# Attention in float32 by head pairs on halves of TensorE's rows and columns, with a float32 first input product in batch 0

## The chip, the cores and the metric

The kernel runs on one core of one Trainium2 chip. The metric is the time of one execution on the device, in microseconds. The time of before is 1350.27 us, the median of three runs (1349.99 to 1351.18).

## The reference

There are 4 batches, 12 heads, a sequence of 448 and a head size of 64. For each head:

```python
scores = scale * np.matmul(q, k.transpose(0, 1, 3, 2))
scores = cap * np.tanh(scores / cap)
scores = scores - np.max(scores, axis=-1, keepdims=True)
attn = np.exp(scores)
attn = attn / (np.sum(attn, axis=-1, keepdims=True) + 1e-09)
out = np.matmul(attn, v)
```

The heads' outputs side by side are a matrix x of 1792 rows and 768 columns. Two layers follow, each with an input product (768 to 2048), a pointwise function and an output product (2048 to 768): `h - tanh(h)` in the first, `h * sigmoid(1.702 h)` in the second. Activations come as float32, the weights as float64. The result is float32.

## The kernel before, in words

Everything is kept transposed: features on the 128 partitions, the 448 positions of a batch along the free dimension. The kernel works batch by batch. `attention()` (L491) is a generator over all 48 heads that stops at each batch's end; the loop at L723 goes through the products of one batch (`moe`, L680: input and output product of layer one, then of layer two) and after each matrix product counts up `owed` by the rates of L32, and takes a step of the attention of the next batch whenever a full step is owed (L730 to L734). In the first quarter of batch 0's products the rate is 0. Batch 0's own attention runs alone before it (L709). The program is then put in order per engine by a scheduler, which keeps this priority but lets work go ahead that is ready, such as weight conversions during batch 0's attention.

**Precision.** TensorE multiplies either float32 or a rounded form of it that takes fewer passes. The kernel mostly uses the rounded form three times: a number is split into a high part (`hi_act`, `hi_dve`, L93 to L97) and the rest (`lo_dve`, `lo_pool`, L99 to L103), and high by high, high by low and low by high are added up. So `gemm_in` (L619) makes 18 products of 128 x 128 by 128 x 448 for each of its 16 blocks f, and `gemm_out` (L640) 48 for each of its 6 blocks e. A block of `gemm_in` takes its PSUM bank from the pool `ps_m` (two banks), in later batches every fourth from `ps_s` (L622).

**Weights.** In batch 0 each of 68 chunks of weights comes as float64 (`dbl_dma`, L159, three buffers `wd`), is made float32 by two steps of ScalarE and two of VectorE (`w_convert`, L189, three buffers `wr`), is written back to HBM for later batches (`kept`, L203), and is split into `wh` and `wl` (`w_split`, L206, three buffers each): the high part on VectorE or ScalarE, the low part on GpSimd in batch 0 and on VectorE later. `ahead` (L573) asks for the chunk that is needed two blocks later.

**Attention before.** A pair g is two heads. `load_qk` (L238) and `load_v` (L250) load it. For pairs 0 and 1 `pt_head` (L263) transposes q and k of each head to 64 rows of float32, and `qk` (L323) makes the scores in float32. For all other pairs q and k are transposed, split into high and low (`th`, `tl`, L289 and L290), and put on top of each other by 12 transfers (`pt_stack`, L292: `qs`, `kh`, `kl`), so that two products over 128 rows give the scores of one chunk of 112 queries. `tanh_max` (L345) takes the tanh and the row maximum of two chunks; `exps` (L362) makes the exponentials, with row sums from the same instruction; `norm` (L372) divides, on VectorE and GpSimd, except in batch 0, where the division is left for the output. `p_trans` (L394) transposes the probabilities and copies them (`pf`) in batch 0 or splits them (`ph`, `pl`) later. `pv` (L422) multiplies by v: in batch 0 in float32, both heads on halves of TensorE's columns; later by eight products per head, with v split by `v_split` (L312). `pv_out` (L447) writes x, in batch 0 with its split (`xh`, `xl`, L463 and L464). PSUM tiles of attention come from `ps_b` (two tiles of two banks, and a third from `ps_f` in batch 0, L130) and from `ps_s` (two banks).

## Time and profile before

| | |
|---|---|
| median of three runs | 1350.27 us |
| the profiled execution | 1349.97 us |
| its span (first to last instruction) | 1348.2 us |
| TensorE busy in the span | 1265.4 us, 94% |
| VectorE / ScalarE / GpSimd busy | 950.5 / 911.1 / 383.9 us |
| mean granted TensorE clock | 0.976 of 2.4 GHz |
| moved by DMA | 235 MB, 174 GB/s |

The span is what the profile sees of the execution. An engine's busy share is a mean over stages that differ much. Matrix products overlap, and their ends are modelled, so that the mean duration of one (370 ns for 448 columns) is longer than the distance to the next.

### The profile page before, as it was taken

To read this page: it belongs to the slowest core of one execution; us is meant where nothing else is said; L and a number is where in the kernel's file an instruction comes from. 1 tells how busy PE (TensorE), PEld (TensorE's weight loads), DVE (VectorE), ACT (ScalarE), POOL (GpSimd) and SP (SyncE) were. 2 spreads that over 40 slices of the span, in tenths; PEclk is the share of its full clock that TensorE was granted. 3 is DMA by queue.
4 is the path that set the end of the run, shared out by engine and by line. 5 is a ranking of instruction groups with operands and counts; after the bars stand their busy time and mean duration, and the time that the engine had idled before them with its cause. 6 is when DMAs were issued, how large, how long until landed. Compare 5 with 4: busy or idle time off the path is not lost.

```text
span 1348.2 us, 19078 instructions
## 1 busy us (share of the span) xinstructions
PE 1265.4 (94%) x6484; PEld 1109.9 (82%) x6484; DVE 950.5 (70%) x1338; ACT 911.1 (68%) x1466; POOL 383.9 (28%) x298
## 2 busy tenths in 40 slices
PE   8988778889888899999999999999999999999998
PEld 4556666778777788799999999999999999999997
DVE  5787999877888869976677727976767528834432
ACT  6986788888889869766777627866666527633421
POOL 1103556445674333310133102310132003201300
PEclk7999899899999899999999999999999999999999
DMA  7675556887778778665555566555543367433342
GB/s 202 169 180 149 174 168 212 240 269 238 205 251 244 216 229 300 250 184 152 142 150 140 158 186 204 149 149 143 151 133 109 96 181 215 130 116 112 105 118 59
DMA packets 170225, 235.23 MB, mean 174 GB/s; under 512 B 14224, under 2 KB 127120, under 8 KB 170128
## 3 DMA queue, kind: packets, MB, share of 16 engines
q1 hardware_dynamic: 170128, 234.02, 58.4%
q8 instruction: 51, 0.84, 0.3%
q14 instruction: 46, 0.38, 0.1%
HBM read 157.68 MB, written 46.01 MB: 151 GB/s over the span
## 4 chain that ended last, share of the span: by engine, by line
PE 61%; ACT 3%; DVE 3%; DMA 2%; issue 1%; SPq 1%; DVEq 0%; ACTq 0%
PE ps_y L648 27%; PE ps_h L628 23%; PE ps_pv L441 3%; PE ps_sc L339 3%; PE ps_pt L408 3%; DMA kept<-wr 1%; PE ps_o L671 1%; ACT wd L197 1%; PE ps_qk L279 1%; ACT t L367 0%; DMA wd<-in_moe_w_out_dram 0%; ACT wh L94 0%; DVE wl L100 0%; DMA wr<-kept 0%; DVE wr L199 0%
## 5 line engine op out<-in xcount | busy, mean ns | idle before, releaser
L628 PE MATMUL ps_h<-xh,wh 128*128 128x448 f32 x768 | 287.4, 374 | 37.3 <-DVE g_far L585 20.7
L648 PE MATMUL ps_y<-gh,wh 128*128 128x448 f32 x768 | 284.2, 370 | 7.3 <-DVE gh L97 2.4
L628 PE MATMUL ps_h<-xl,wh 128*128 128x448 f32 x768 | 285.7, 372 | 2.3 <-DVE xl L100 2.3
L648 PE MATMUL ps_y<-gl,wh 128*128 128x448 f32 x768 | 286.3, 373 | 0.2 <-POOL gl L103 0.2
L100 DVE TENSOR_TENSOR wl<-wr,wh 128x768 fp32r<-128x768 f32 (+1 forms) x172 | 157.8, 920 | 156.2 <-PE ps_y L648 84.5
L94 ACT CAST wh<-wr 128x768 fp32r<-128x768 f32 (+1 forms) x195 | 153.1, 787 | 158.6 <-PE ps_y L648 111.7
L628 PEld LDWEIGHTS ps_h<-xh,wh 128*128 128x128 f32 x768 | 146.4, 191 | 58.5 <-DVE g_far L585 24.4
L648 PE MATMUL ps_y<-gh,wl 128*128 128x448 f32 x768 | 188.6, 372 | 0.0
L628 PE MATMUL ps_h<-xh,wl 128*128 128x448 f32 x768 | 185.2, 371 | 0.0
L103 POOL TENSOR_TENSOR wl<-wr,wh 128x768 fp32r<-128x768 f32 (+1 forms) x68 | 130.4, 1918 | 136.1 <-DVE wh L97 82.0
L367 ACT ACTIVATE t<-t,tm,cpos 112x448 f32<-112x448 f32 x192 | 144.5, 756 | 34.5 <-DVE tm L358 34.3
L103 POOL TENSOR_TENSOR gl<-g_q,gh 128x448 fp32r<-128x448 f32 x64 | 90.4, 1413 | 262.0 <-ACT gh L94 166.8
L648 PEld LDWEIGHTS ps_y<-gh,wh 128*128 128x128 f32 x768 | 145.1, 189 | 20.5 <-DVE gh L97 2.7
L628 PEld LDWEIGHTS ps_h<-xl,wh 128*128 128x128 f32 x768 | 146.5, 191 | 15.4 <-DVE xl L100 2.8
L628 PEld LDWEIGHTS ps_h<-xh,wl 128*128 128x128 f32 x768 | 145.4, 191 | 12.7 <-DVE wl L100 0.4
L648 PEld LDWEIGHTS ps_y<-gh,wl 128*128 128x128 f32 x768 | 145.3, 191 | 12.1
L648 PEld LDWEIGHTS ps_y<-gl,wh 128*128 128x128 f32 x768 | 145.3, 189 | 12.0 <-POOL gl L103 0.7
L103 POOL TENSOR_TENSOR gl<-g_g,gh 128x448 fp32r<-128x448 f32 x64 | 79.6, 1244 | 199.5 <-DVE gh L97 66.1
L354 DVE TENSOR_REDUCE tm<-t 112x2 f32<-112x896 f32 x96 | 102.9, 1080 | 42.6 <-ACT t L350 42.3
L390 POOL TENSOR_SCALAR t<-t,rr 112x448 f32<-112x448 f32 x72 | 68.2, 957 | 215.2 <-DVE rr L377 162.6
L350 ACT ACTIVATE t<-ps_sc,tsc 112x896 f32<-112x896 f32 x96 | 95.8, 1010 | 48.0 <-PE ps_sc L339 43.7
L197 ACT ACTIVATE wd<-wd 128x768 uint16<-128x768 uint16 (+1 forms) x68 | 125.6, 1851 | 0.5
(84 smaller groups left out, 1909.5 us busy)
## 6 DMA issues: line engine op xcount, KB each, us to landing
wr<-kept SPq DMA_DIRECT2D x100, 384.0 KB, 3.2
wd<-in_moe_w_in_dram SPq DMA_DIRECT2D x64, 384.0 KB, 4.4
wr<-kept SPq DMA_DIRECT2D x72, 320.0 KB, 2.9
wd<-in_moe_w_out_dram SPq DMA_DIRECT2D x48, 384.0 KB, 4.5
kept<-wr SPq DMA_DIRECT2D x44, 384.0 KB, 5.0
wh<-kept_hl SPq DMA_DIRECT2D x32, 384.0 KB, 3.3
wl<-kept_hl SPq DMA_DIRECT2D x32, 384.0 KB, 3.7
kh<-th SPq DMA_DIRECT2D x88, 112.0 KB, 2.3
```

Of the source, the lines that this page charges most:

```text
L94: nc.scalar.copy(out=dst, in_=src)
L100: nc.vector.tensor_tensor(out=dst, in0=src, in1=hi.bitcast(F32), op=ALU.subtract)
L103: nc.gpsimd.tensor_tensor(out=dst, in0=src, in1=hi.bitcast(F32), op=ALU.subtract)
L197: nc.scalar.mul(out=half[:, :, :, 2], in_=half[:, :, :, 1], mul=F64_LOW)
L339: nc.tensor.matmul(ps[:, i, :S], qs[:, j, c * CP:(c + 1) * CP], kk[:, j, :], start=(m == 0), stop=(m == 1),)
L350: nc.scalar.activation(out=t[:, 2 * half:2 * half + 2], in_=sc_t.pop((n, half))[:, :, :S], func=AF.Tanh, scale=tsc[:CP],)
L354: nc.vector.tensor_reduce(out=tm_t[n][:, 2 * half:2 * half + 2], in_=t[:, 2 * half:2 * half + 2], axis=AX.X, op=ALU.max)
L367: nc.scalar.activation(out=t[:, c], in_=t[:, c], func=AF.Exp, scale=cpos[:CP], bias=tm_t[n][:, c:c + 1], accum_out=ss_t[n][:, c:c + 1],)
L390: nc.gpsimd.tensor_scalar(out=t[:, c], in0=t[:, c], scalar1=rr[:, c:c + 1], scalar2=0.0, op0=ALU.mult, op1=ALU.add)
L408: nc.tensor.transpose(ps[:, i, c * CP:(c + 1) * CP], t[:, c, kc * CP:(kc + 1) * CP], ident[:CP, :CP])
L628: nc.tensor.matmul(ps[:, :S], w[:, kk, :], x[kk], start=(m == 0), stop=(m == len(seq) - 1))
L648: nc.tensor.matmul(ps[:, :S], w[:, f - f0, :], x[f], start=(c == 0 and m == 0), stop=(c == len(parts) - 1 and m == len(seq) - 1),)
```

## The change

Attention becomes float32 throughout and goes by pairs and query chunks of 112 instead of by heads. `prep` transposes q and k of both heads together, head 0 on partitions 0 to 63 and head 1 on 64 to 127, and copies them. `pair_qk` makes the scores of a chunk for both heads, each over its half of the rows. `tanh_max` and `exps` work on one chunk of both heads. `pair_trans` transposes and copies the probabilities, on VectorE in batch 0 and in turn on VectorE and ScalarE later. `pair_pv` multiplies by v in float32, both heads on halves of the columns, in two halves with a step of the generator between them from batch 1 on. In batches 0 and 1 the division moves to the output (`spread`, `r_rows`), in batches 2 and 3 it stays on the probabilities. The stacking transfers, the split of v and the split of the probabilities go. In batch 0 the first layer's input product is made of float32 weights and float32 x (`xf`), 6 products for each block instead of 18, without a split; every second block there takes its bank from `ps_s`. The steps owed per batch become 60 instead of 84. The output leaves in one transfer per block instead of two. Buffers change with this. The removed bodies of the attention functions stand above and are left out here.

```diff
-QK_F32_PAIRS = 2
-HEADS_AHEAD = 2
+AHEAD = 2
...
-    rv_p = pool("rawv", 1)
-    vs_p = pool("vs", 1)
-    th_p = pool("thl", 1)
-    st_p = pool("stk", 2)
-    t_p = pool("t", 2)
-    sm_p = pool("small", 2)
+    rv_p = pool("rawv", 2)
+    qk_p = pool("qk", 2)
+    t_p = pool("t", 4)
+    sm_p = pool("small", 4)
+    rw_p = pool("rw", 1)
...
-    xh = [big.tile([P, S], F32R, name=f"xh{i}") for i in range(KM)]
+    xf = [big.tile([P, S], F32, tag=f"xh{i}", name=f"xf{i}") for i in range(KM)]
+    xh = [None] * KM
     xl = [big.tile([P, S], F32R, name=f"xl{i}") for i in range(KM)]
     first = ExitStack()
-    t_f = first.enter_context(tc.tile_pool(name="t_f", bufs=2))
-    ph_f = first.enter_context(tc.tile_pool(name="ph_f", bufs=1))
-    th_f = first.enter_context(tc.tile_pool(name="th_f", bufs=1))
-    r_f = first.enter_context(tc.tile_pool(name="r_f", bufs=2))
+    t_f = first.enter_context(tc.tile_pool(name="t_f", bufs=4))
     wz_f = first.enter_context(tc.tile_pool(name="wz_f", bufs=1))
-    raw_f = first.enter_context(tc.tile_pool(name="raw_f", bufs=1))
+    raw_f = first.enter_context(tc.tile_pool(name="raw_f", bufs=2))
...
             r = w_convert(i) if i < NCH else raws.pop(i)
+            if i < KF:
+                whl[i] = (r, None)
+                n_split[0] += 1
+                continue
...
-        t = (raw_f if g < NP and g % 2 else raw_p).tile([CP, 2, 2, C * D], F32, tag="raw", name="raw")
+        t = (raw_f if g < NP and g % 3 else raw_p).tile([CP, 2, 2 * C * D], F32, tag="raw", name="raw")
         for i, src in enumerate((q, k)):
-            last_raw[0] = nc.sync.dma_start(
-                out=t[:, i], in_=src[b, 2 * hp:2 * hp + 2].rearrange("h (p c) d -> p h (c d)", c=C)
-            )
+            for j in range(2):
+                last_raw[0] = nc.sync.dma_start(
+                    out=t[:, i].rearrange("p (c e) -> p c e", c=C)[:, :, j * D:(j + 1) * D],
+                    in_=src[b, 2 * hp + j].rearrange("(p c) d -> p c d", c=C),
+                )
...
+    def prep(g, i):
         t = raw[g]
+        if i == 0:
+            qkt[g] = qk_p.tile([P, 2, S], F32, tag="qk", name="qk")
+        else:
+            raw.pop(g)
+        ps = ps_s.tile([P, 512], F32, tag="s", name="ps_qk")
+        for c in range(C):
+            nc.tensor.transpose(ps[:, c * CP:(c + 1) * CP], t[:, i, c * P:(c + 1) * P], ident[:CP, :CP])
+        (hi_act if i == 1 and g >= NP else hi_dve)(qkt[g][:, i], ps[:, :S])
+    def pair_qk(g, c):
+        ps = big_ps(g, "ps_sc")
+        for j in range(2):
+            a = slice(j * D, (j + 1) * D)
+            nc.tensor.matmul(
+                ps[:, j, :S], qkt[g][a, 0, c * CP:(c + 1) * CP], qkt[g][a, 1], start=True, stop=True
+            )
+        sc_t[g, c] = ps
+    def tanh_max(g, c):
+        t = tt[g, c] = (t_f if g < NP and c % 2 else t_p).tile([CP, 2, S], F32, tag="t", name="t")
+        tm = tm_t[g, c] = sm_p.tile([CP, 2], F32, tag="tm", name="tm")
+        nc.scalar.activation(out=t, in_=sc_t.pop((g, c))[:, :, :S], func=AF.Tanh, scale=tsc[:CP])
+        nc.vector.tensor_reduce(out=tm, in_=t, axis=AX.X, op=ALU.max)
+        nc.vector.tensor_scalar(out=tm, in0=tm, scalar1=cneg[:CP], scalar2=None, op0=ALU.mult)
+    def exps(g, c):
+        t, tm = tt[g, c], tm_t.pop((g, c))
+        whole = g < 2 * NP
+        if c == 0 or not whole:
+            ss_t[g] = sm_p.tile([CP, 2, C], F32, tag="ss", name="ss")
+        ss = ss_t[g]
+        for j in range(2):
+            nc.scalar.activation(
+                out=t[:, j], in_=t[:, j], func=AF.Exp, scale=cpos[:CP],
+                bias=tm[:, j:j + 1], accum_out=ss[:, j, c:c + 1],
+            )
+        if whole:
             return
+        ss_t.pop(g)
+        at = ss[:, :, c]
+        nc.vector.tensor_scalar(out=at, in0=at, scalar1=EPS, scalar2=None, op0=ALU.add)
+        nc.vector.reciprocal(out=at, in_=at)
+        nc.vector.tensor_scalar(out=t[:, 0], in0=t[:, 0], scalar1=ss[:, 0, c:c + 1], scalar2=None, op0=ALU.mult)
+        nc.gpsimd.tensor_scalar(
+            out=t[:, 1], in0=t[:, 1], scalar1=ss[:, 1, c:c + 1], scalar2=0.0, op0=ALU.mult, op1=ALU.add
+        )
+    def spread(g):
+        ss = ss_t.pop(g)
+        nc.vector.tensor_scalar(out=ss, in0=ss, scalar1=EPS, scalar2=None, op0=ALU.add)
+        nc.vector.reciprocal(out=ss, in_=ss)
+        rw[g] = rw_p.tile([CP, C, 2, D], F32, tag="rw", name="rw")
+        for j in range(2):
+            nc.gpsimd.tensor_copy(out=rw[g][:, :, j], in_=ss[:, j].unsqueeze(2).to_broadcast([CP, C, D]))
+    def r_rows(g):
+        w = rw.pop(g)
+        ps = ps_s.tile([P, 512], F32, tag="s", name="ps_r")
+        for c in range(C):
+            nc.tensor.transpose(
+                ps[:, c * CP:(c + 1) * CP], w[:, c].rearrange("p j d -> p (j d)"), ident[:CP, :CP]
+            )
+        return ps
+    def pair_trans(g, c):
+        t = tt.pop((g, c))
+        if c == 0:
+            p_t[g] = ph_p.tile([CP, C, 2, S], F32, tag="p", name="pf")
+        ps = big_ps(g, "ps_pt")
+        for kc in range(C):
+            for j in range(2):
+                o = (2 * (kc % 2) + j) * CP
                 nc.tensor.transpose(
+                    ps[:, kc // 2, o:o + CP], t[:, j, kc * CP:(kc + 1) * CP], ident[:CP, :CP]
                 )
+        (hi_act if c % 2 and g >= NP else hi_dve)(
+            p_t[g].rearrange("p (i k) j s -> p i (k j) s", i=2)[:, :, :, c * CP:(c + 1) * CP],
+            ps[:, :, :S].rearrange("p i (m s) -> p i m s", s=CP),
+        )
+    def pair_pv(g, half):
+        if half == 0:
+            r_t[g] = ps_s.tile([P, 512], F32, tag="s", name="ps_pv")
+        for kc in (2 * half, 2 * half + 1):
+            for j in range(2):
+                nc.tensor.matmul(
+                    r_t[g][j * D:(j + 1) * D, :S], rawv[g][:, j, kc, :], p_t[g][:, kc, j, :],
+                    start=(kc == 0), stop=(kc == C - 1),
+                )
+    def pair_out(g):
+        hp = g % NP
+        ps = r_t.pop(g)
+        for d in (p_t, rawv, qkt):
+            d.pop(g)
+        x = xs_p.tile([P, S], F32, tag="xs", name="xs")
+        if g < 2 * NP:
+            pr = r_rows(g)
+        nc.scalar.copy(out=x, in_=ps[:, :S])
+        if g < NP:
+            nc.vector.tensor_tensor(out=xf[hp], in0=pr[:, :S], in1=x, op=ALU.mult)
             return
+        if g < 2 * NP:
+            nc.vector.tensor_tensor(out=x, in0=pr[:, :S], in1=x, op=ALU.mult)
+        n_pair[0] = hp + 1
+        xst[hp] = x
+        if not x_free[0]:
             nc.sync.dma_start(out=xd[hp], in_=xst.pop(hp))
...
+        for i in range(2):
+            prep(0, i)
+            yield False
+        load_qk(2)
+        units = [(g, c) for g in range(NP) for c in range(C)]
+        for u in units[:AHEAD]:
+            pair_qk(*u)
+            tanh_max(*u)
+            yield False
+        for n, (g, c) in enumerate(units):
+            exps(g, c)
+            for u in units[n + AHEAD:n + AHEAD + 1]:
+                pair_qk(*u)
+                tanh_max(*u)
+            yield False
+            if c < 2:
+                if g + 1 < NP:
+                    prep(g + 1, c)
+                    if c == 1 and g + 3 < NP:
+                        load_qk(g + 3)
+                if g > 0:
+                    if c == 0:
+                        spread(g - 1)
+                        pair_pv(g - 1, 0)
+                        pair_pv(g - 1, 1)
+                    else:
+                        pair_out(g - 1)
+                        yield False
+            if c == 2:
+                load_v(g + 1)
+            pair_trans(g, c)
+            yield False
+        load_qk(NP)
+        spread(NP - 1)
+        pair_pv(NP - 1, 0)
+        pair_pv(NP - 1, 1)
+        pair_out(NP - 1)
+        yield True
+        for i in range(2):
+            prep(NP, i)
+            yield False
+        load_qk(NP + 1)
+        def softmax(g, c):
+            tanh_max(g, c)
+            exps(g, c)
+        for g in range(NP, NG + 1):
+            for c in (0, 1):
+                if g < NG and g % NP:
+                    if c == 0:
+                        pair_qk(g, 0)
+                        pair_qk(g, 1)
+                        yield False
+                    softmax(g, c)
+                if g > NP:
+                    pair_trans(g - 1, 2 + c)
+                    yield False
+            if g > NP:
+                if g - 1 < 2 * NP:
+                    spread(g - 1)
+                for half in range(2):
+                    pair_pv(g - 1, half)
+                    if half:
+                        pair_out(g - 1)
+                    yield half == 1 and g % NP == 0
+            if g == NG:
+                break
+            load_v(g + 1)
+            if g % NP == 0:
+                pair_qk(g, 0)
+                pair_qk(g, 1)
                 yield False
+                softmax(g, 0)
+                softmax(g, 1)
+            pair_qk(g, 2)
+            pair_qk(g, 3)
+            yield False
+            for c in (0, 1):
+                softmax(g, 2 + c)
+                pair_trans(g, c)
                 yield False
+            if g + 1 < NG:
+                for i in range(2):
+                    prep(g + 1, i)
+                    yield False
+                load_qk(g + 2)
...
-            if b > 0 and f % 4 == 3:
+            if f % 4 == 3 if b > 0 else layer == 0 and f % 2:
                 ps = ps_s.tile([P, 512], F32, tag="s", name="ps_h")
             else:
                 ps = ps_m.tile([P, 512], F32, tag="m", name="ps_h")
             seq = [p for kk in range(KM) for p in ((wh, xh, kk), (wh, xl, kk))] + [(wl, xh, kk) for kk in range(KM)]
+            passes = 1
+            if wl is None:
+                seq = [(wh, xf, kk) for kk in range(KM)]
+                passes = 3
             for m, (w, x, kk) in enumerate(seq):
                 nc.tensor.matmul(
                     ps[:, :S], w[:, kk, :], x[kk], start=(m == 0), stop=(m == len(seq) - 1)
                 )
                 if m == 0:
                     ahead(i)
-                if m == LATE_AT:
+                if m == LATE_AT // passes:
                     run_late()
-                if m < len(seq) - 1:
+                for _ in range(passes - (m == len(seq) - 1)):
...
+                if b == 0:
+                    xh[e] = big.tile([P, S], F32R, tag=f"xh{e}", name=f"xh{e}")
...
-        o = ob_p.tile([CP, C, P], F32, tag="o", name="o")
-        nc.vector.tensor_copy(out=o.rearrange("p c e -> p (c e)"), in_=ps[:CP, :])
-        dst = out[b * S:(b + 1) * S, e * P:(e + 1) * P].rearrange("(p cc s) e -> p s cc e", cc=2, s=2)
-        for s in range(2):
-            nc.sync.dma_start(out=dst[:, s], in_=o[:, 2 * s:2 * s + 2, :])
+        o = t_p.tile([CP, 2, S], F32, tag="t", name="o").rearrange("p a s -> p (a s)")[:, :C * P]
+        nc.vector.tensor_copy(out=o, in_=ps[:CP, :])
+        o = o.rearrange("p (c e) -> p c e", c=C)
+        dst = out[b * S:(b + 1) * S, e * P:(e + 1) * P]
+        nc.sync.dma_start(out=dst.rearrange("(p c) e -> p c e", c=C), in_=o)
...
-    per_batch = 7 * H
+    per_batch = 10 * NP
```

## Rows read from the trace of the kernel before

**Rows 1.** Busy time by stage; columns: us, each engine's busy us, PEclk, DMA

```profile
0.00:117.50 117.50, 103.83 (x519) 59.98 (x520) 82.87 (x136) 93.08 (x171) 11.66 (x21) 0.91 0.71 191
117.50:202.30 84.80, 64.92 (x281) 55.08 (x280) 81.59 (x96) 66.28 (x92) 46.80 (x28) 0.94 0.48 149
202.30:295.00 92.70, 81.02 (x412) 71.67 (x411) 82.70 (x103) 80.38 (x107) 49.84 (x33) 0.96 0.77 241
295.00:396.00 101.00, 84.32 (x416) 74.22 (x415) 83.76 (x107) 86.74 (x119) 63.24 (x42) 0.92 0.73 227
396.00:505.00 109.00, 97.48 (x511) 85.90 (x512) 86.55 (x120) 90.03 (x132) 47.86 (x34) 0.95 0.78 233
505.00:1342.00 837.00, 833.08 (x4347) 762.64 (x4345) 532.29 (x779) 494.00 (x847) 164.48 (x142) 1.00 0.52 154
```

**Rows 2.** Waits, 117.5 to 202.5 us: us in total, times, longest

```profile
PE ps_h L628 <- DVE g_far L585: 19.9, 13, 3.2
```

**Rows 3.** VectorE and GpSimd groups, 117.5 to 202.5 us

```profile
L198 DVE TENSOR_SCALAR wr<-wr 128x768 uint32<-128x768 uint32 x11 | 15.4, 1397 | 0.0
L97 DVE CAST wh<-wr 128x768 fp32r<-128x768 f32 x8 | 6.0, 753 | 2.4 <-PE ps_h L628 2.4
...
L103 POOL TENSOR_TENSOR wl<-wr,wh 128x768 fp32r<-128x768 f32 x13 | 26.9, 2072 | 12.4 <-DVE wh L97 8.4 <-issue 2.4 <-PE ps_h L628 1.3
```

**Rows 4.** VectorE groups, 0 to 117.5 us

```profile
L97 DVE COPY pf<-ps_pt 112x896 f32<-112x896 f32 x24 | 25.9, 1083 | 2.4 <-PE ps_pt L408 2.4
...
L100 DVE TENSOR_TENSOR tl<-ps_qk,th 128x448 fp32r<-128x448 f32 x12 | 7.4, 618 | 0.0
...
L198 DVE TENSOR_SCALAR wr<-wr 128x768 uint32<-128x768 uint32 x6 | 3.2, 556 | 2.7 <-ACT wr L196 2.7
```

**Rows 5.** ScalarE groups, 0 to 117.5 us

```profile
L197 ACT ACTIVATE wd<-wd 128x768 uint16<-128x768 uint16 x6 | 11.4, 1945 | 0.0
...
L94 ACT CAST th<-ps_qk 128x448 fp32r<-128x448 f32 x12 | 6.5, 540 | 2.3 <-PE ps_qk L279 2.3
...
L196 ACT ACTIVATE wr<-wd 128x768 f32<-128x768 f32 x6 | 5.4, 916 | 1.9 <-DMA wd<-in_moe_w_in_dram 1.9
```

**Rows 6.** PE in order of time: start, us, instructions

```profile
33.95 3.26 PE L330 MATMUL ps_sc<-khf,qsf 64*112 64x448 f32 x8
...
40.56 1.72 PE L431 MATMUL ps_pv<-pf,rv 112*64 112x448 f32 x8 [0.39 <-DVE pf L97]
42.21 0.66 PE L339 MATMUL ps_sc<-kh,qs 128*112 128x448 f32 x2
42.81 1.72 PE L431 MATMUL ps_pv<-pf,rv 112*64 112x448 f32 x6
44.45 0.60 PE L456 MATMUL ps_r<-ident,rw 112*128 112x112 f32 x4
...
55.47 0.97 PE L431 MATMUL ps_pv<-pf,rv 112*64 112x448 f32 x4 [1.34 <-DVE pf L97]
```

**Rows 7.** TensorE groups, 0 to 117.5 us

```profile
L431 PE MATMUL ps_pv<-pf,rv 112*64 112x448 f32 x96 | 27.8, 586 | 6.4 <-DVE pf L97 5.2 <-DVE tl L100 1.2
```

**Rows 8.** The chain that ended last, a piece of 288 products

```profile
1163.92 58.53 PE ps_y L648 x288
```

**Rows 9.** ScalarE groups, 202.3 to 505 us

```profile
L94 ACT CAST ph<-ps_pt 112x896 fp32r<-112x896 f32 x25 | 23.1, 926 | 1.6 <-PE ps_pt L408 1.5
L94 ACT CAST th<-ps_qk 128x448 fp32r<-128x448 f32 x12 | 6.6, 554 | 0.0
```

**Rows 10.** VectorE groups, 202.3 to 505 us

```profile
L100 DVE TENSOR_TENSOR pl<-ps_pt,ph 112x896 fp32r<-112x896 f32 x25 | 27.1, 1083 | 3.7 <-ACT ph L94 3.6
L386 DVE TENSOR_SCALAR t<-t,rr 112x448 f32<-112x448 f32 x24 | 18.3, 798 | 0.3
```

**Rows 11.** DMA issues: count, KB each, median us to landing

```profile
kh<-th SPq DMA_DIRECT2D x88, 112.0 KB, 2.3
...
raw<-in_q_dram SPq DMA_DIRECT2D x24, 224.0 KB, 3.0
```

281 lines of the change are left out of this document (7 added, 274 removed).

## The prediction

> **What bounds the kernel now.** I read the busy time by stage first, because the page's average mixes stages with different limits [rows 1]. The stage borders are the places where batch 0's products start in earnest (117.5 us), where its first input product ends (202.3), where its first output product ends (295) and where its second input product ends (396), the end of batch 0's products (505), and the last product (1342). After 505 us TensorE is busy for 833 of 837 us and nobody else is above 64%: there the time is the sum of TensorE's work, and what other engines gain is worth nothing. Before 505 us no engine is full in the long run. I call the stages A (0 to 117.5, attention of batch 0 alone), B (117.5 to 202.3, first input product of batch 0), C (202.3 to 505, the rest of batch 0 with the attention of batch 1 between) and D (505 to 1342).
>
> In A ScalarE is the busiest that does its work at its own speed, 93 of 117.5 us; the 104 us of TensorE contain waiting inside modelled ends and slices at the lower clock (granted 0.91 on average). In B VectorE is full, 81.6 of 84.8 us, and the longest wait of TensorE is for VectorE to release a product's bank, 19.9 us in 13 waits [rows 2]. VectorE is not only busy but slowed: the shift of a weight chunk (L198) takes 1397 ns in B [rows 3] and 556 ns in A [rows 4], and what has come in is GpSimd, with 13 subtractions `wl` of 2.07 us [rows 3]. In C ScalarE (257 of 302.7 us) and VectorE (253) are about level [rows 1], so the stage needs both to lose work.
>
> **The change, stage by stage.** Prices on TensorE first. A rounded-float product of 448 columns costs 58.53 / 288 = 0.203 us [rows 8]. A float32 product appears as two records (the 48 value products of batch 0 are 96 records [rows 7]). Eight records on the two column halves take 1.72 us and four take 0.97 us [rows 6], so two records, one on each half, share a slot of (1.72 - 0.97) / 2 = 0.375 us. Eight records on one row half alone take 3.26 us, (3.26 - 1.72) / 4 = 0.385 us each [rows 6]: without a partner a record has a slot for itself. Going in and out of halves costs something too: from 40.56 to 42.21 us is 1.65 us for four slots (1.50), and the two rounded products behind take 0.60 us up to 42.81 instead of 0.41 [rows 6]. That is 0.15 + 0.19 = 0.34 us for each block of such work.
>
> No row of before has two row halves at work together, as the new scores do. Bounds: 0.375 us per two records (as the columns), or 0.75 us (as a row half alone). I take 0.375, because the nearest row with two tiles is that of the columns, and because the two heads of a chunk write to different banks. The column row shows a full factor of two. The Trainium skill (TensorE: Matmul & The Clock Gate, section "Measured speedup vs the span model") has four row strips at 3.07 times, not four, which no run here shows; by it the sum would come out 11 us higher, an estimate.
>
> *Stage D*, twelve pairs (batches 2 and 3). Removed per pair: 16 score and 16 value products, 32 x 0.203 = 6.50 us. Added: 8 + 8 float32 products, 32 records in 16 slots, 6.00 us, in four blocks (two of two score chunks, two value halves that a yield separates), 4 x 0.34 = 1.36 us. Net +0.86 us, twelve times **+10**. Transposes are as many as before. Bounds: -6 (no price for a block) and +18 (the score chunks apart, six blocks). ScalarE and VectorE lose work here (no high and low parts of weights on the probabilities, no split of v), under a full TensorE, so at no gain.
>
> *Stage A.* ScalarE loses 12 casts `th` (6.5 us), six casts of x, of the same size (3.2), and four half copies (2) [rows 5]. It also loses three of the six weight conversions that were done early, 3 x (1.95 + 0.92) = 8.6 us [rows 5]: the first 16 chunks now stay in the three `wr` buffers until used, so only three can be ahead. Those move to B. VectorE loses 12 `tl` (7.4 us) and six `xl` of that size (3.7), and gets 12 copies of q and k of that size (7.4); its 24 copies `pf` stay [rows 4]. TensorE's work hardly changes: pairs 2 to 5 had 3.25 us of scores and get 3.0 + 4 x 0.34 = 4.36 (each chunk is a block of its own here), pairs 0 and 1 fall from 16 x 0.375 = 6.0 to 4.36; together +1 us. Bounds: 0 (TensorE's chain through the six pairs sets the end) and -26 (the stage shrinks as ScalarE's load, 20.3 of 93.1 us). I take the middle, **-13**, since both loads are close and the look-ahead shrinks from four chunk-halves to two chunks. The loads of q and k become four transfers per pair in place of two, in pieces of a quarter of the size; the 12 stacking transfers per pair (88 issues of this one kind [rows 11]) go. Only the first pair's load is exposed: between nothing and one more landing, 3.0 us [rows 11]; I take nothing, since the pieces go out one behind the other. Later loads are issued a pair ahead, behind attention's work of over 10 us.
>
> *Stage B.* TensorE: 96 float32 products, 192 x 0.375 = 72.0 us, in place of 288 x 0.203 = 58.5; the stage took 84.8. VectorE loses the `wh` casts (6.0 us) and the slowing by `wl` (11 shifts at 1397 against 556 ns: 9.3 us, and as much again on the other steps) [rows 3, 4]; it falls below 65 us. The wait for a bank [rows 2] goes too, as odd blocks now use the other pool. Late next is TensorE itself (72), with ScalarE close (66.3 of before, less some casts, plus the 8.6 us moved here). Bounds: -12 (TensorE alone) and +4 (ScalarE's chain of conversions); **-6**.
>
> *Stage C.* ScalarE loses `ph` (23.1 us) and `th` (6.6), and gets half of the 24 probability copies, 12 x 0.93 = 11.1, and six copies of k, 3.3 [rows 9]; the casts of v go as well: about -16. VectorE loses `pl` (27.1) and the scaling of the probabilities (18.3), and gets 12 copies of 1.08 us, 13.0 [rows 10]: -32, and GpSimd's half of the scaling goes. TensorE gets 6 x 0.86 us and 24 transposes of about 0.1 us [rows 6]: +7.6, on 176 us of products, 39 of attention and 240 transposes (24), together 247. If the stage follows ScalarE it shrinks by 302.7 x 16 / 257 = 19; I take **-20** (283, TensorE 87% full). Bounds: -4 (the weight pipeline sets it) and -36 (it follows VectorE).
>
> Sum: -13 - 6 - 20 + 10 = -29. The profiled execution took 1349.97 us (span 1348.2), 0.3 below the median, so **1321 us**.
>
> **The rivals.**
> - *Row halves in turn*, the slower side. If two float32 products on row halves don't run together (the form 64*112 is in the trace only alone [rows 6]), a pair's scores need 16 slots: +3.0 us. That decides in D, where nothing hides it: +36. In C TensorE's 247 become 265 of 283, so some 12 of the 20 are lost; in A, with 18 us more, the gain turns into +2. 1321 + 36 + 12 + 15 = 1384 us. Also what would come if the compiler put both heads on the same rows. Anything above about half of this price makes the kernel slower. Against: the columns' factor of two.
> - *Row halves that overlap in part*: between the bounds of 0.375 and 0.75 us per two records [rows 6] the value 0.49 gives 3.9 us for a pair's scores, +0.9 per pair, +11 in D: 1332 us. For it: nothing shows row halves at the full factor. Against it: the columns have it. The Trainium skill's 3.07 of 4 (same page and section) stands on this rival's side.
> - *The early stages don't shrink*, because the conversion of the weights sets them: transfers are busy for 0.73 to 0.78 in C [rows 1], and each chunk still needs 1.95 us of one ScalarE step [rows 5]. A -5, B 0, C -5, D +10: 1350 us, no change. For: the conversions per chunk are the same. Against: GpSimd's `wl` stops in B, and VectorE's load in C falls by an eighth.
> - *More than the sum*: VectorE's freed time and shorter chains let C follow VectorE (-36), A -20, B -10, and blocks cost half in D (+5): 1289 us.
>
> **How the numbers follow.** Chances: forecast 0.57, row halves in turn 0.11, in part 0.10, early stages don't shrink 0.12, more 0.10. About 0.2% is what a measurement can tell from no change here. Faster: 0.57 + 0.10 + 0.10 and a third of the fourth, 0.81; same 0.05; slower 0.14, the first rival and a rest of the fourth. The range leaves out the first rival and half of the last one: 1292 to 1352 us; the likeliest case alone lies within 1300 to 1340.
>
> **What would show it.** In the profile after: score products of 64 rows starting in twos, 0.375 us from two to two (right), or each 0.375 us behind the last (first rival). Stage D longer by about 10 us with TensorE still full; if TensorE has waits of over 5 us there, the sum of D is wrong. First product of batch 0 at full pace near 104 us; stage B near 79 us with no long wait for `g_far` and VectorE's shift near 0.6 us; stage C near 283 us. If C stays at 300 us with TensorE waiting for weights, the conversion pipeline was the bound. The forecast is wrong if the halves don't pair, or if less than 10 us come out of the first 505.

## The result, and the profile after

The changed kernel takes **1361.72 us** (median of four runs, 1359.95 to 1364.77) beside 1350.72 us for the kernel before on the same chip: a ratio of 1.0079, with a 95% interval of 1.0059 to 1.0099. The forecast was 1321 us. It is slower by 0.8%, in a direction to which the forecast gave 14 in 100, and outside the range of 1292 to 1352.

The profiled execution of after took 1359.95 us, its span 1358.2 us, so 10.0 us more than the span of before. The busy time by stage, with the borders where the same work starts or ends (first product of batch 0, which now runs at full pace at once; end of its first input product; end of its first output product; end of its second input product; end of batch 0's products; last product), answers to [rows 1]; columns as there.

```profile
0.00:99.40 99.40, 83.92 (x469) 42.73 (x470) 69.26 (x114) 70.36 (x133) 5.18 (x18) 0.95 0.40 109
99.40:172.00 72.60, 72.32 (x194) 36.28 (x192) 64.45 (x91) 68.09 (x96) 19.90 (x13) 1.00 0.68 211
172.00:275.50 103.50, 85.92 (x397) 68.33 (x398) 70.55 (x97) 82.01 (x106) 42.10 (x25) 0.90 0.76 243
275.50:375.30 99.80, 82.99 (x406) 66.66 (x405) 67.25 (x88) 76.29 (x99) 49.86 (x34) 0.95 0.61 192
375.30:489.00 113.70, 97.20 (x527) 72.67 (x526) 61.51 (x93) 76.39 (x110) 31.99 (x24) 0.98 0.57 175
489.00:1352.00 863.00, 855.80 (x4409) 725.02 (x4407) 496.01 (x783) 464.23 (x795) 176.42 (x144) 1.00 0.44 131
```

| stage | before [rows 1] | after | difference | forecast |
|---|---|---|---|---|
| A | 117.5 | 99.4 | -18 | -13 |
| B | 84.8 | 72.6 | -12 | -6 |
| C | 302.7 | 317.0 | **+14** | **-20** |
| D | 837.0 | 863.0 | **+26** | **+10** |
| sum | | | +10 | -29 |

A and B gained more than was forecast. All of it went, and more, in C and D. In C the odd thing is the rest of the row: ScalarE is busy for 234.7 of 317 us (257 of 302.7 before) and VectorE for 199.3 (253 before). ScalarE lost 22 us, where the prediction said 16, and VectorE 54, where it said 32, and the stage is longer all the same; TensorE's busy time there is 266 against 263 us, so it stands still for 51 us against 40. What does the stage wait for? The waits of stage C that bear on it (us in total, times, longest):

```profile
ACT wr L192 <- POOL wl L101: 40.3, 19, 4.3
POOL wl L101 <- PE ps_y L568: 24.5, 5, 6.0
PE ps_pt L339 <- ACT t L286: 13.1, 6, 4.9
PE ps_h L548 <- DVE g_g L532: 11.9, 6, 3.1
ACT wr L192 <- DMA kept<-wr: 8.5, 6, 2.5
PE ps_sc L278 <- ACT qk L92: 7.6, 3, 2.8
PE ps_y L568 <- DVE wh L95: 3.4, 2, 3.2
```

In stage C of before the same step of ScalarE and the same transposes of TensorE had these as their longest:

```profile
ACT wr L196 <- DMA kept<-wr: 4.5, 3, 1.8
...
PE ps_pt L408 <- ACT t L350: 0.3, 1, 0.3
```

The first line of after is new. ScalarE's first conversion step (L192, it writes `wr`) waits 40.3 us for a `wr` buffer that GpSimd's `wl` has still to read; in before it waited 4.5 us, for the write-back. TensorE, for its part, waits little for weights (the last line of after, 3.4 us): its longest wait is for ScalarE's tanh, 13.1 us, which was 0.3. A stretch of the time line of after (ScalarE, TensorE, GpSimd: start, us, instruction, in brackets the idle time ahead of it and what ended it) shows how the two belong together:

```profile
259.96 1.76 PE L278 MATMUL ps_sc<-qk 64*112 64x448 f32 x8
260.23 0.90 ACT L192 ACTIVATE wr<-wd 128x768 f32<-128x768 f32 x1 [1.48 <-POOL wl L101]
261.45 1.95 ACT L193 ACTIVATE wd<-wd 128x768 uint16<-128x768 uint16 x1
...
265.04 1.81 POOL L101 TENSOR_TENSOR wl<-wr,wh 128x768 fp32r<-128x768 f32 x1 [4.84 <-DVE wh L95]
...
266.89 0.89 ACT L192 ACTIVATE wr<-wd 128x768 f32<-128x768 f32 x1 [3.48 <-POOL wl L101]
267.81 1.90 ACT L193 ACTIVATE wd<-wd 128x768 uint16<-128x768 uint16 x1
269.46 1.89 ACT L286 ACTIVATE t<-ps_sc,tsc 112x896 f32<-112x896 f32 x2
270.51 1.74 PE L339 MATMUL ps_pt<-ident,t 112*112 112x112 f32 x8 [4.94 <-ACT t L286]
...
272.44 0.57 PE L568 MATMUL ps_y<-gh,wh 128*128 128x448 f32 x1
272.82 0.57 PE L568 MATMUL ps_y<-gl,wh 128*128 128x448 f32 x1
```

Two chunks of scores are ready at 261.7 us. ScalarE has their tanh behind a weight conversion in its order, and that conversion waits until 266.9 for GpSimd to let go of a buffer. So the tanh starts at 269.46, 7.7 us after the scores; the transposes of the pair before need the PSUM bank that the tanh frees, and TensorE stands still for 4.94 us. It pays twice, as the windows of this stretch show:

```profile
255.50:265.40 9.90, 9.90 (x51) 7.77 (x49) 4.67 (x7) 6.39 (x7) 2.11 (x2) 1.00 0.69 210
265.40:270.50 5.10, 0.16 (x1) 0.00 (x0) 1.32 (x2) 3.58 (x4) 1.45 (x1) 0.77 0.99 333
270.50:275.40 4.90, 4.89 (x18) 4.55 (x19) 3.02 (x6) 3.91 (x9) 1.81 (x1) 0.54 0.88 281
```

The granted clock is 1.00 while TensorE is busy, and 0.54 in the 4.9 us behind its idle stretch (the lower of its two levels, 1.2 GHz, is 0.50); the products at 272.44 and 272.82 stand 0.38 us apart where 0.20 is the rule [rows 8].

On TensorE itself the float32 halves do what the forecast took. The time line of attention in batch 0 (start, us, instructions) answers to [rows 6]:

```profile
62.18 0.93 PE L339 MATMUL ps_pt<-ident,t 112*112 112x112 f32 x8
63.04 1.01 PE L278 MATMUL ps_sc<-qk 64*112 64x448 f32 x4
63.98 0.98 PE L339 MATMUL ps_pt<-ident,t 112*112 112x112 f32 x8
```

Four score records on two row halves take 1.01 us, and the eight at 259.96 above take 1.76, so two records, one on each half, share a slot of (1.76 - 1.01) / 2 = 0.375 us, as on the column halves. From start to the next start four records take 0.94 us (63.04 to 63.98): two such slots, and 0.19 for going in. One after the other they would have needed 1.5. And stage B, groups of instructions in 99.4 to 172 us (busy, mean ns, idle before), which answer to [rows 2, 3]:

```profile
L548 PE MATMUL ps_h<-xf,wr 128*128 128x448 f32 x192 | 72.3, 539 | 0.0
L194 DVE TENSOR_SCALAR wr<-wr 128x768 uint32<-128x768 uint32 x14 | 7.7, 551 | 0.2 <-ACT wr L192 0.2
```

TensorE is full with its 192 records, no wait for a bank is left, and VectorE's shift takes 551 ns where it took 1397 beside GpSimd's `wl`.

### The profile page after: what moved, and what is told of

The parts are those of the page before. It is cut to its first block, busy times and chain, and to the rows that moved or that the text cites. A ratio compares the mean times of both kernels' runs of the same rounds, so it can differ in the third digit from the quotient of the medians.

```text
span 1358.2 us, 18305 instructions
## 1 busy us (share of the span) xinstructions
PE 1278.9 (94%) x6396; PEld 1012.1 (75%) x6396; DVE 829.7 (61%) x1262; ACT 837.9 (62%) x1334; POOL 325.5 (24%) x258
## 4 chain that ended last, share of the span: by engine, by line
PE 59%; DVE 6%; ACT 5%; issue 2%; DMA 1%; POOL 1%; SPq 0%; DVEq 0%; ACTq 0%; POOLq 0%
PE ps_y L568 28%; PE ps_h L548 20%; PE ps_pv L352 4%; PE ps_pt L339 3%; PE ps_sc L278 3%; ACT wd L193 1%; DVE g_q L514 1%; DVE g_q L515 1%; ACT t L297 1%; POOL wl L101 1%; DVE g_t L512 1%; ACT wr L192 1%; PE ps_o L593 1%; DMA wd<-in_moe_w_out_dram 1%; PE ps_qk L271 1%
## 5 line engine op out<-in xcount | busy, mean ns | idle before, releaser
L568 PE MATMUL ps_y<-gl,wh 128*128 128x448 f32 x768 | 289.5, 377 | 1.0 <-POOL gl L101 1.0
L548 PE MATMUL ps_h<-xh,wh 128*128 128x448 f32 x672 | 252.0, 375 | 19.4 <-DVE g_g L532 11.9
L92 ACT CAST wh<-wr 128x768 fp32r<-128x768 f32 (+1 forms) x189 | 148.5, 786 | 187.7 <-PE ps_y L568 139.7
L548 PE MATMUL ps_h<-xl,wh 128*128 128x448 f32 x672 | 251.1, 374 | 0.2 <-DVE xl L98 0.2
L548 PE MATMUL ps_h<-xh,wl 128*128 128x448 f32 x672 | 160.8, 370 | 0.0
L548 PEld LDWEIGHTS ps_h<-xh,wh 128*128 128x128 f32 x672 | 128.4, 191 | 38.9 <-DVE g_g L532 14.6
L548 PEld LDWEIGHTS ps_h<-xl,wh 128*128 128x128 f32 x672 | 128.4, 191 | 13.6 <-issue 2.7
L548 PEld LDWEIGHTS ps_h<-xh,wl 128*128 128x128 f32 x672 | 125.2, 189 | 16.9 <-issue 6.8
L101 POOL TENSOR_TENSOR wl<-wr,wh 128x768 fp32r<-128x768 f32 (+1 forms) x52 | 94.4, 1817 | 148.0 <-DVE wh L95 55.7
L339 PE MATMUL ps_pt<-ident,t 112*112 112x112 f32 x768 | 94.9, 266 | 22.2 <-ACT t L286 13.1
L286 ACT ACTIVATE t<-ps_sc,tsc 112x896 f32<-112x896 f32 x96 | 93.3, 1001 | 34.7 <-PE ps_sc L278 31.7
```

What stands on the lines that cost most here:

```text
L92: nc.scalar.copy(out=dst, in_=src)
L101: nc.gpsimd.tensor_tensor(out=dst, in0=src, in1=hi.bitcast(F32), op=ALU.subtract)
L286: nc.scalar.activation(out=t, in_=sc_t.pop((g, c))[:, :, :S], func=AF.Tanh, scale=tsc[:CP])
L339: nc.tensor.transpose(ps[:, kc // 2, o:o + CP], t[:, j, kc * CP:(kc + 1) * CP], ident[:CP, :CP])
L548: nc.tensor.matmul(ps[:, :S], w[:, kk, :], x[kk], start=(m == 0), stop=(m == len(seq) - 1))
L568: nc.tensor.matmul(ps[:, :S], w[:, f - f0, :], x[f], start=(c == 0 and m == 0), stop=(c == len(parts) - 1 and m == len(seq) - 1),)
```

## The experiments

Theory 1, which the time line suggests: ScalarE works in a fixed order; with its loads gone its conversions go ahead until no buffer is free, and then hold up the attention that stands behind them. Theory 2: the first chunks, which are no longer split, hold the three `wr` buffers, so that too few conversions are ahead when stage C begins. Theory 3: the transposes wait for the tanh, whatever the conversions do. Theory 4 came with the second set of runs: ScalarE's waits are slack, and TensorE's short waits and lower clock set the stage. (In the last run the expectation uses this number for another thought, a stall in batch 1.) Stage lengths of the profiled executions, by the end of the first input product, the end of batch 0's products and the last product (A and B together, since the border between them means another thing in each kernel):

| kernel | time, us | ratio to before | A+B | C | D |
|---|---|---|---|---|---|
| before | 1350 to 1352 | | 202.3 | 303.0 | 836.9 |
| after | 1361.72 | 1.0079 | 171.7 | 316.9 | 863.5 |
| attention alone | 1380.67 | 1.0211 | 196.9 | 312.0 | 864.1 |
| float32 first product alone | 1352.61 | 1.0006 | 187.2 | 313.9 | 842.2 |
| five `wr` buffers | 1360.76 | 1.0070 | 176.9 | 313.4 | 864.0 |
| tanh early | 1362.76 | 1.0075 | 173.6 | 317.5 | 864.0 |
| conversions behind attention | 1334.20 | 0.9860 | 170.4 | 290.0 | 862.6 |
| the same, one block ahead | 1342.11 | 0.9919 | 170.5 | 295.3 | 867.5 |
| `wl` on VectorE | 1338.23 | 0.9895 | 175.6 | 294.6 | 862.1 |
| value halves in one block | 1352.23 | 1.0001 | 172.7 | 314.6 | 858.7 |
| before, conversions behind attention | 1349.82 | 1.0001 | 208.0 | 304.5 | 837.1 |
| both edits | 1328.60 | 0.9834 | 174.0 | 289.6 | 859.6 |
| both, quiet first product | 1327.89 | 0.9826 | 174.1 | 289.9 | 859.1 |

A+B of one profile is not exact to better than some 5 us (see the last section); C and D repeat within 1 to 3 us where nothing touches them.

### Attention alone, and the first product alone

The first kernel is after with the first product in rounded passes again (the split of x in batch 0, `wh` and `wl` of the first 16 chunks and the banks of before come back); the second is before with the float32 product and its two bank pools.

Attention alone, against after:

```diff
-            if i < KF:
-                whl[i] = (r, None)
...
+            hi_act(xh[hp], x)
+            lo_dve(xl[hp], x, xh[hp])
```

> The new attention, with the first input product of batch 0 in three rounded passes again (x split after pair_out, weights split, banks as before). Theory 1 (the new attention's own order slows the rest of batch 0: ScalarE, which works in order, stands before a weight conversion whose wr buffer is not free, and the tanh behind it is late): the stretch from the end of the first input product to the end of batch 0 stays at 312 us or more (317 in the changed kernel), total near 1368 us (A -18, B 0, C +12, D +24). Theory 2 (the unsplit first chunks hold the three wr buffers, so that fewer conversions are ahead when the stretch begins): that stretch falls to 290 to 303 us, total near 1352 us.

The first product alone, against before:

```diff
+            if i < KF:
+                whl[i] = (r, None)
...
+            if wl is None:
+                seq = [(wh, xf, kk) for kk in range(KM)]
+                passes = 3
```

> The kernel before with the float32 first input product of batch 0 alone (and its second bank pool); attention as before. Theory 1: stretch B falls from 85 to about 73 us, the rest of batch 0 stays at 303 us (+-4) and D at 837, total near 1338 us. Theory 2: B falls as well, but the rest of batch 0 rises to 312 us or more, total 1348 to 1355 us.

Attention alone is slower by 2.1% (1.0177 to 1.0245): D carries the whole +27 us, A and B gain only 5 us, and C has the wait of `wr` behind `wl` as after has it (40.3 us there):

```profile
ACT wr L191 <- POOL wl L101: 41.3, 21, 4.3
```

So neither the wait nor D's loss needs the first product, and theory 2, which had C between 290 and 303 us here, falls for the changed kernel. (The total is 13 us above what theory 1 had, because A and B gained 5 us and not 18.) The first product alone is neither faster nor slower (0.9988 to 1.0023): the 15 us that A and B gain come back as 11 us in C and 5 in D. These are the numbers that theory 2 had for this kernel, but not its reason: TensorE waits for weights for 3.4 us in C. Nor is it the new wait; the waits of its stage C are

```profile
PE ps_sc L344 <- DVE pl L100: 14.0, 8, 5.6
...
ACT wr L197 <- POOL wl L103: 2.7, 2, 1.4
```

so scores wait for a bank that VectorE's `pl` must read, 5.5 us more than in before (8.5), with a granted clock of 0.92 over the stage (0.94 in before, the mean of the three rows in [rows 1]). The parts don't add up: by medians they are worth +30 and +1 us alone and +11 together. What else holds up C of the first product alone, and what its D lost, was not followed further.

### More buffers

```diff
-    wr_p = pool("wraw", 3)
+    wr_p = pool("wraw", 5)
```

> The changed kernel with five wr buffers instead of three. Theory 1 and theory 2 both have ScalarE's conversion wait for GpSimd's release of wr (40 us in the rest of batch 0): it falls below 15 us, that stretch from 317 to 300 us or less, total 1345 us or less. Theory 3 (the stretch is long because transposes wait for the tanh that has to free their bank, whatever the conversions do): the stretch stays within 5 us of 317, total 1357 to 1365 us.

The time is that of after within its scatter. The waits of stage C say why:

```profile
ACT wr L192 <- POOL wl L101: 37.1, 21, 4.1
POOL wl L101 <- PE ps_y L568: 35.4, 11, 5.7
```

Two more buffers let the conversions get two chunks further (the count is in the section on the conversions behind attention), and then they wait for the same thing. GpSimd now waits 35.4 us for TensorE's products to give back `wl` (24.5 in after). That TensorE's own use of the weights stands at the end of that chain, whatever the number of `wr`, is argued from this wait: GpSimd waits longer still, 42.8 us, for VectorE's high parts. Theory 1 had the wait of `wr` fall below 15 us, and it did not. The numbers are those of theory 3 (C within 5 us of 317, 1357 to 1365 us in all), whose own reason the next run tests. The number of buffers is not the cause; what is left of theory 1 is the place of the conversions in ScalarE's order.

### The tanh earlier in the program

The tanh of a chunk is issued right behind its scores, ahead of the second chunk's.

```diff
                         pair_qk(g, 0)
+                        tanh_max(g, 0)
                         pair_qk(g, 1)
+                        tanh_max(g, 1)
                         yield False
-                    softmax(g, c)
+                    exps(g, c)
```

> The changed kernel with each chunk's tanh and maximum issued right behind its scores, ahead of the step's end, from batch 1 on; exponentials stay where they are. Theory 3: TensorE's waits of the transposes for the tanh (13 us in all) fall below 4 us, the rest of batch 0 falls from 317 by 8 us or more, total 1350 to 1354 us. Theory 1: the blocked conversions remain ahead of the exponentials, the stretch falls by less than 5 us, total 1356 to 1363 us.

Nothing moved; stage C's waits are those of after:

```profile
ACT wr L192 <- POOL wl L101: 40.5, 20, 4.3
PE ps_pt L339 <- ACT t L286: 12.3, 6, 5.4
```

So the tanh is not late because of its own place in the program, and theory 3 falls: it had this wait below 4 us and the stage 8 us shorter.

### Conversions behind attention

From chunk 19 on, the two conversion steps on ScalarE are put in its order behind the tanh or exponential that was issued last. No work is added or left out, and no buffer changes.

```diff
+        with ExitStack() as behind:
+            if i > KF + 2:
+                behind.enter_context(tc.issue_after(att_act[0].ins))
             nc.scalar.mul(out=o, in_=high.bitcast(F32), mul=2.0 ** -112)
             nc.scalar.mul(out=half[:, :, :, 2], in_=half[:, :, :, 1], mul=F64_LOW)
...
-        nc.scalar.activation(out=t, in_=sc_t.pop((g, c))[:, :, :S], func=AF.Tanh, scale=tsc[:CP])
+        att_act[0] = nc.scalar.activation(
+            out=t, in_=sc_t.pop((g, c))[:, :, :S], func=AF.Tanh, scale=tsc[:CP]
+        )
...
```

> The changed kernel, with ScalarE's two conversion steps of a chunk (from chunk 19 on) held behind the tanh and the exponentials that were issued ahead of them; in ScalarE's order two to three fewer conversions then stand before each tanh of batch 1. Theory 1 (conversions placed too far ahead in ScalarE's order wait there for a wr buffer and hold up the attention behind them): ScalarE's wait for GpSimd's wl falls from 40 to about 20 us, the rest of batch 0 from 317 to 305 us or less, total 1350 us or less. Theory 4 (these waits are slack that ScalarE has anyway, and TensorE's chain of short waits and lower clock sets the stretch): the waits move, the stretch stays within 5 us of 317, total 1357 to 1365 us.

1334.2 us, 0.9860 of before (0.9835 to 0.9886), and 27 us less than after, all of it in C. The same scores as in the time line above, in this kernel's:

```profile
260.66 1.91 ACT L291 ACTIVATE t<-ps_sc,tsc 112x896 f32<-112x896 f32 x2 [0.86 <-PE ps_sc L283]
...
265.07 0.92 ACT L197 ACTIVATE wr<-wd 128x768 f32<-128x768 f32 x1
```

Now ScalarE waits for the scores, as it should, and the conversion comes behind the exponentials. The waits of its stage C and the busy times of the stage (columns as [rows 1]):

```profile
ACT wr L197 <- DMA kept<-wr: 12.5, 9, 2.9
...
PE ps_pt L346 <- ACT t L291: 1.3, 1, 1.3
```

```profile
170.50:461.00 290.50, 258.92 (x1328) 201.59 (x1328) 217.64 (x276) 233.11 (x313) 125.09 (x83) 0.97 0.70 219
```

The wait behind `wl` is gone from the list, TensorE's wait for the tanh fell from 13.1 to 1.3 us, and the granted clock of the stage rose from about 0.94 to 0.97. ScalarE's work is the same, 233 us against 235. Of the 27 us, 19.5 are time in which TensorE stands still (51.2 us in C of after, 31.7 here), and 7.5 are products that take less time at the higher clock (265.8 and 258.3 us busy). The run ahead itself can be counted in the traces. When TensorE starts a chunk of stage C, ScalarE has begun the conversion of so many later chunks, on the mean: 1.5 in before, 3.0 in after, 4.9 with five `wr` buffers, 2.0 here. This is what shows theory 1: the order alone is worth 27 us.

### How far back

The same, and weights of batch 0's later chunks asked for one block ahead in place of two:

```diff
-        w_split(i + 2)
+        w_split(i + (1 if KF < i < NCH else 2))
```

> The same, and in the rest of batch 0 a chunk is converted one block ahead instead of two: one conversion fewer again before each tanh. Theory 1: a further fall of ScalarE's wait for wl to about 10 us and of the stretch by 4 us or more, as long as TensorE doesn't wait for weights; total 1346 us or less. Theory 4: no fall; if conversions come late now, TensorE's waits for weights rise and the total goes above 1362 us.

1342.1 us: 8 us worse than two blocks ahead. Theory 1 had stage C 4 us shorter; it is 5 us longer, and so is D, which was not followed. In C TensorE now waits for the high parts of weights (`wh`, 9.5 us, 3.5 with two blocks). Too early and too late both cost; the run ahead is needed, but not ahead of attention.

### The low parts on VectorE

If the `wr` buffer is given back sooner, the order should matter less. GpSimd's `wl` of batch 0 goes to VectorE.

```diff
-            (lo_pool if i < NCH else lo_dve)(l[:, :n], r[:, :n], h[:, :n])
+            lo_dve(l[:, :n], r[:, :n], h[:, :n])
```

> The changed kernel with the low parts of batch 0's weights made on VectorE (about 1 us each) instead of GpSimd (1.8 us). Theory 1: wr is released earlier, ScalarE's wait for it falls below 20 us, and the rest of batch 0 falls from 317 to 305 us or less. Theory 4: VectorE, with 118 us free in that stretch, takes the 50 us, and the stretch stays within 6 us of 317.

1338.2 us, 0.9895 (0.9871 to 0.9919): C fell to 294.6 us without any change of ScalarE's order. The waits:

```profile
ACT wr L192 <- DVE wl L98: 25.0, 17, 3.6
...
PE ps_pt L339 <- ACT t L286: 6.1, 4, 2.4
```

The wait behind `wl` is shorter (25.0 us, where theory 1 had below 20), and TensorE's wait for the tanh halves with it. That the two go together, by another way than the order, speaks for theory 1. It does not show it by itself: with `wl` gone from GpSimd VectorE's own conversion step (L195, 768 columns) also fell from 1184 to 958 ns, and no run parts the two.

### The kernel before with the same order

The edit of the conversions behind attention, in the kernel before:

```diff
+            if i > KF + 2:
+                behind.enter_context(tc.issue_after(att_act[0].ins))
```

> The kernel before with the one edit that made the changed kernel fast: ScalarE's weight conversions from chunk 19 on stand behind the tanh or exponential of attention that was last issued. Theory 1 (it is the change that makes conversions run ahead until they wait for a buffer): the kernel before shows no wait of ScalarE for a weight buffer behind GpSimd's low part in stage C, so there is nothing to remove: stage C stays within 4 us of 301.5 and the time within 1347 to 1355 us. Rival (the held conversions are worth as much to any kernel of this kind): stage C near 291 us and the time at or below 1341 us, and then the change itself is worth only the rest, some 5 to 10 us. Third possibility (the kernel before needs the conversions that early): TensorE waits for weights by over 5 us in stage C and the time is above 1355 us.

A ratio of 1.0001 (0.9983 to 1.0019), C 304.5 us: nothing to be had. In stage C of the kernel before no conversion waits for GpSimd's `wl`; it is the change that made the order a bound. That the load of ScalarE and VectorE is what kept the conversions back there is argued, not shown: the new attention also has another order of steps, and no run changes the load alone. The other way round: with the order put right, the change as such is worth 1.4%.

### Value halves in one block

```diff
+                yield False
                 for half in range(2):
                     pair_pv(g - 1, half)
-                    if half:
-                        pair_out(g - 1)
-                    yield half == 1 and g % NP == 0
+                pair_out(g - 1)
+                yield g % NP == 0
```

> The changed kernel with both halves of a pair's value products in one block from batch 1 on: 18 blocks fewer, of which 12 fall after batch 0. If a block costs what the trace of before shows, 0.34 us, the time after batch 0 falls from 869 by 4 us, to about 865, and the total to 1356 to 1358 us. If the extra 27 us after batch 0 come mainly from blocks (more than 1 us each), it falls by 12 us or more. If they come from stalls and moved work, it changes by less than 2 us.

D is shorter by 4.8 us (863.5 to 858.7), for one block less in each of twelve pairs: 0.40 us a block. The same edit on top of the conversions behind attention, in the next section, takes 3.0 us from D (862.6 to 859.6), 0.25 us a block. The 0.34 that the prediction read from [rows 6] lies between. The profiled span is 6.1 us shorter than after's (D -4.8, C -2.3, A and B +1.0); the medians differ by 9.5, more than the 4 to 6 that were expected, and what is beyond 6 has no place in these traces.

### Both edits, and a quiet first product in batch 1

The conversions behind attention and the value halves in one block together:

```diff
+                behind.enter_context(tc.issue_after(att_act[0].ins))
...
+                yield False
                 for half in range(2):
                     pair_pv(g - 1, half)
```

> Conversions held behind attention and both value halves of a pair in one block. If the two gains lie in different places (stage C, and the blocks of batches 1 and 2), they add: 1334.2 less 4.9, 1329 us, stages of batches 1 and 2 at 313 and 305.5 us, stage C within 2 us of 290.6. If the larger steps of attention disturb stage C, whose TensorE is no longer idle as often, stage C comes to 293 us or more and the time to 1332 us or more.

1328.6 us, **0.9834 of before** (0.9809 to 0.9860): the gains add, as far as four and five runs can tell (1329 us was expected), C 289.6 and D 859.6 us. On top of this, batch 1's first input product, in which TensorE waits 4.8 us for `g_far` (L501 of after), was kept free of attention:

```diff
-ATT_RATES = {"first": (0.0, 0.7, 0.7, 1.3), "last": (0.3, 1.1, 0.7, 1.1), "mid": (0.3, 0.9, 0.9, 0.8)}
+ATT_RATES = {"first": (0.0, 0.7, 0.7, 1.3), "last": (0.3, 1.1, 0.7, 1.1), "mid": (0.0, 1.1, 1.1, 0.8)}
```

> As the run with both edits, and batch 1's first input product gets no step of attention (rates 0.0, 1.1, 1.1, 0.8 in place of 0.3, 0.9, 0.9, 0.8). Theory 4 (part of the loss after 489 us is a stall of the first input product of batch 1, where VectorE has that product's pointwise steps and attention's steps in one order): the 4.8 us wait of TensorE for g_far goes, and with it the stretch at half clock behind it (6.8 us); batch 1 shrinks from 313 to between 303 and 307 us and the time by 6 to 10 us against the run with both edits. Rival (TensorE's work alone sets batch 1, and the first product only pays where it carries attention): the first product shrinks, the later quarters grow by as much, and batch 1 and the time stay within 2 us. Other end: the later quarters now have waits for attention of their own, and the time is longer by over 2 us.

1327.9 us against 1328.6, no difference. The windows of that first product and of the rest of batch 1, first with both edits, then with the quiet product:

```profile
464.60:540.90 76.30, 71.49 (x351) 60.80 (x350) 67.07 (x106) 60.57 (x108) 24.01 (x18) 0.96 0.73 243
540.90:778.90 238.00, 238.00 (x1278) 195.41 (x1277) 127.41 (x215) 126.01 (x219) 44.50 (x39) 1.00 0.40 114
```

```profile
465.10:531.50 66.40, 63.08 (x311) 55.13 (x309) 56.28 (x80) 48.91 (x84) 16.70 (x13) 1.00 0.81 275
531.50:778.40 246.90, 244.93 (x1317) 198.34 (x1316) 138.72 (x240) 137.23 (x242) 51.79 (x43) 1.00 0.39 111
```

The first product is 9.9 us shorter and the rest 8.9 longer, as the rival said (TensorE's work alone sets batch 1); the gain of 6 to 10 us did not come. The lower clock (0.96 in the first row) went, but not the waiting: TensorE waits 5.3 us in this batch 1, 3.3 of it for `g_far` and 1.9 for the tanh, in place of the one wait of 4.8. So the rates gain nothing; what a batch 1 without a stall would gain is not shown, because the waits moved and did not go. These last two are the fastest kernels of the study.

## Why the prediction was wrong

**Row halves.** Right: two float32 products on row halves share a slot of 0.375 us. Both rivals built on the opposite fall. The Trainium skill (TensorE: Matmul & The Clock Gate, section "Measured speedup vs the span model") has 3.07 for four row strips of 32; two halves of 64 rows reach the full factor of two here, so the 11 us more by that figure did not come.

**Stage A**, -13 said, -18 measured, within its bounds; the place where the border lies is uncertain by some 5 us. ScalarE lost 22.7 us there (20.3 said). **Stage B**, -6 said, -12 measured: the lower bound (TensorE alone, 72.0 us) was the right value, to 0.6 us. The steps behind it were right one by one: VectorE below 65 us (64.5), no long wait for `g_far`, the shift at 551 ns. ScalarE, close at 68.1 us, was not a bound.

**Stage C** is the step that failed: "If the stage follows ScalarE it shrinks by 302.7 x 16 / 257 = 19". The loads fell, and by more than forecast (ScalarE -22, VectorE -54 us; -16 and -32 were said). But the stage did not follow a load. ScalarE was idle for 82 of 317 us and still late with the tanh, because prefetch work stands in its fixed order and the tanh behind it waits wherever the prefetch waits: 40.3 us behind GpSimd's `wl`, where before had none. No bound given for C allowed a loss. (The bound that follows VectorE should read -38, 302.7 x 32 / 253, and not -36; nothing hangs on it.) The prediction's rule for being wrong looked for "TensorE waiting for weights": the weights were early, and the attention behind them was late. With the order put right C takes 290 us: -12 to -13, in the direction and within the bounds that were given, two thirds of the size. The rival "the early stages don't shrink" came nearest by its time, 1350 us, but not by its reason: A and B did shrink, and conversions were not slow, but too early.

**Stage D**, +10 said, +26 measured, outside its bounds of -6 to +18, is the second step that failed: "Net +0.86 us, twelve times **+10**" left out a term. The term for pairs was about right: by 0.25 to 0.40 us a block, 6.0 + 4 x (0.25 to 0.40) - 6.50 is 0.5 to 1.1 us per pair, 6 to 13 in all. What was missing is work that crossed the border at the end of batch 0. The groups of TensorE in D of after, then of before:

```profile
L339 PE MATMUL ps_pt<-ident,t 112*112 112x112 f32 x389 | 46.1, 262 | 0.0
L352 PE MATMUL ps_pv<-pf,rv 112*64 112x448 f32 x208 | 44.6, 551 | 0.0
L278 PE MATMUL ps_sc<-qk 64*112 64x448 f32 x192 | 42.3, 559 | 0.9 <-ACT qk L92 0.9
```

```profile
L408 PE MATMUL ps_pt<-ident,t 112*112 112x112 f32 x369 | 43.2, 259 | 0.0
L339 PE MATMUL ps_sc<-kh,qs 128*112 128x448 f32 x88 | 32.2, 366 | 0.0
L339 PE MATMUL ps_sc<-kl,qs 128*112 128x448 f32 x88 | 32.1, 365 | 0.0
```

Twelve pairs have 192 score products; the kernel before made only 176 of them in D, the other 16 (3.2 us at 0.203) in C, where TensorE had room. After makes all 192 records (twelve pairs of 16) in D, and 208 value records where twelve pairs have 192: half-slots of 0.375 / 2, so 3.0 us of batch 1's last pair slipped over. With 20 more transposes of probabilities, 8 of q and k (88 and 80) and 4 of row sums, of about 0.11 us each (the eight at 62.18 take 0.86 us to the next start), that is some 10 us. The prediction compared pair with pair and not the place of the pairs: it should have counted what the look-ahead of the kernel before and the order of the yields put on either side of 505 us. That leaves 3 to 10 of the 26. TensorE waits 7.2 us in D of after and 3.9 in before; the prediction had named waits of over 5 us as the sign that its sum of D is wrong. The longest is the one of 4.8 us in batch 1's first product, with the lower clock behind it. The quiet first product moved these waits and gained nothing, so what they cost, and the rest, stays open.

**The sum.** The prediction said it would be wrong if less than 10 us came out of the first 505; 16 came out. That test was too weak: it left D out, whose rise alone outweighs them.

## What to carry to other kernels

When a change takes load off an engine that also prepares data for later, don't scale its stage with its busy time: ask how far ahead the preparation will now run, on what it will wait when it can go no further, and which urgent instruction stands behind it in that engine's order. Tie the preparation behind the urgent work in the order (not by more buffers), as far as the consumer still gets it in time. And when work is handed out in steps to fill another loop, count per stage which steps fall on either side of a border, above all where the stage behind has no room.

## What the runs showed of the hardware

- In the stretch of stage C shown above, idle TensorE cost more than the idle time: behind 5 us of waiting the granted clock was 0.54 for the next 4.9 us, in which products stand 0.38 us apart and not 0.20.
- Two row halves reach the whole factor of two in float32 (four records take 1.01 us, eight 1.76, so 0.375 us for two), as the column halves do; a block that was saved gave 0.25 us in one pair of kernels and 0.40 in another.
- The start of the kernel was not the same length in two executions. The kernel before and the same with its conversions tied behind attention, an edit that touches only chunks from 19 on, run the same instructions in the same order on TensorE, VectorE, ScalarE and GpSimd up to the first product, and reach it at 107.2 and at 112.9 us, with the same busy times of VectorE (75.2 and 75.3 us) and ScalarE (86.1 and 86.3); the granted clock of that stretch was 0.90 in the one and 0.85 in the other. In the windows by stage the stretches are, of before and of its edited form:

```profile
0.00:107.20 107.20, 93.53 (x461) 53.78 (x462) 75.22 (x123) 86.11 (x157) 11.25 (x20) 0.90 0.70 185
```

```profile
0.00:112.90 112.90, 99.31 (x461) 57.06 (x462) 75.34 (x123) 86.27 (x157) 11.23 (x20) 0.85 0.67 176
```
